# A decode step with grouped attention and a gated feed-forward: another order for the last loads, four strips for wo's last rows

## The chip, the cores and the metric

The kernel runs on one core of a Trainium2 chip. The metric is the device time of one execution in microseconds; each kernel is run several times and the median is given. A profile is one further execution with the hardware profiler on, and its times are counted from the start of its span.

## The reference

One token `x` (512 wide) goes through an attention block with a long cache and through a feed-forward block; a scalar gate mixes the two.

```python
q = x @ wq                                   # 32 heads of 128
k, v = k_cache, v_cache                      # 8 key/value heads, 32768 positions, 128 wide, bf16
scores = einsum(q, k) * 128 ** -0.5          # each k head serves 4 q heads
o = softmax(scores) @ v
a = o.reshape(4096) @ wo                     # wo: 4096 x 512
b = (silu(x @ w_gate) * (x @ w_up)) @ w_down # w_down: 1792 x 512
g = sigmoid((x * gate_w).sum())
out = g * a + (1 - g) * b                    # 512 numbers
```

Nearly all bytes are the two caches: 16 blocks of K and 16 blocks of V, of 4096 KB each.

## The kernel before

**Groups and blocks.** There are G = 8 groups (a key/value head with its four query heads), and each group's 32768 positions are NB = 2 blocks of 16384. Below, K(7,1) is the second block of K of the last group. A block is one DMA into one page of `page`: 128 partitions with 32 KB each. Pages 0 and 2 (`PG_K`) take the two K blocks of a group, pages 1 and 3 (`PG_V`) the V blocks; page 4 (`PG_X`) holds wq at first and wo later.

**TensorE** (line 314 on) first computes q, gate and up from wq, w_gate and w_up. Then a loop (line 509) runs G + 1 times; in turn i it does, for each block b, `emit_k` of group i (line 372: transposes K as 32-bit words into PSUM, DVE copies them to `ktT` at line 639, line 384 computes scores) and `emit_v` of group i - 1 (line 428: the exponentials times V, four at a time, into four strips of PSUM partitions of `ps_o`). `emit_v` of block 0 starts with `emit_reduce` (line 410), which sums the strips of the group before from `acc`, ACT's copy of `ps_o`. In the last turn there is no `emit_k`; between V(7,0) and V(7,1) `emit_warm` (line 466) runs 18 matmuls whose result nobody reads; behind V(7,1) comes `emit_end`.

**The end** (line 468 on): a matmul sums the exponentials, `emit_reduce` the last group. DVE scales (lines 662 to 668), transposes (675), TensorE permutes (479), DVE copies the result to `O2` (677): 32 columns, one for each of the 32 rows j of wo (each row is 128 partitions x 512 outputs). wo comes in five chunks (`WO_CUTS`, rows 0-8, 8-18, 18-26, 26-30, 30-32), each with its semaphore. The rows below `WIDE` = 18 go through `emit_wide` (line 440): one matmul with a stationary column and 512 moving columns, row j into strip j % 4 of `ps_w`. The 14 rows of w_down (with `tT`, the feed-forward's hidden vector, as columns) go the same way, between the first and the second chunk of wo. DVE copies `ps_w` to `part` (683). The remaining 14 rows of wo go through `emit_rows` (line 453), where a row is four matmuls with 128 moving columns each, one for each quarter of the 512 outputs; first the same is done with `part` and a column of ones (`sel5`), which adds up the four strips. The four quarters stand in two strips: each strip has two PSUM rows, and the stationary operand has two columns of which one is zero (`O2z`), so that a matmul adds to its own row and adds zero to the other. DVE casts the result to `res_row` (685), and SP and ACT store two rows of it each (205).

**The order of the loads** is the order in SP's program (line 279 on); all of them stand in one queue. A K block waits until its page's transposes are done (`sem_fill`), a V block until the V block before it in its page has been used (`sem_v_free`). At the end (lines 302 to 310) stand V(7,0), wo's first chunk, V(7,1), w_down, and wo's other four chunks.

Of the kernel before, what the change touches and what calls it, by code (L numbers as in the profile page):

```python
# [13 lines left out]
def bass_gated_mix__gqa_block_cached__swiglu_ffn__decode_kernel(  # L14
# [43 lines left out]
    assert KC * H * DH <= PAGE and 2 * KC * F <= PAGE and WOJ * NOUT <= PAGE  # L58
    WO_CUTS = [0, 8, 18, 26, 30, 32]
    KW = 1  # L60
    WIDE = WO_CUTS[KW + 1]
    NWARM = 18
    OC = NOUT // 128

    RQ = 4
    NSTRIP = 4
    RPS = 2
    assert RQ * HPG <= 32 and RQ * DH == 512

    PG_K = (0, 2)  # L70
# [5 lines left out]
    with ExitStack() as es:  # L76
# [83 lines left out]
        nbias = T("nbias", [128, G, HPG], FP32)  # L160
        esum = T("esum", [128, G, NB, HPG], FP32)
        esum2 = T("esum2", [128, G, HPG], FP32)
        sel5 = T("sel5", [128, 17], FP32)
        sel4 = sel5[:, 1:17]
        acc = T("acc", [128, RQ, DH], FP32)
        oT = T("oT", [128, (G + 2) * STEP], FP32)
        rS = T("rS", [128, H], FP32)
# [1 line left out]
        oTs = T("oTs", [128, H], BF16)  # L169
        O2a = T("O2a", [128, WOJ], BF16)  # L170
        O2 = T("O2", [128, WOJ], BF16)
        O2z = T("O2z", [128, WOJ - WIDE, RPS, RPS], BF16)
        part = T("part", [128, NOUT], FP32)
        res_row = T("res_row", [128, 128], BF16)

# [15 lines left out]
        ps_e = pst[0][:, 0:512]  # L191
        ps_c = pst[1][:, 0:512]
        ps_w = pst[0][:, 512:1024]
        ps_d = pst[1][:, 512:1024]

        def row_view(p):
            return page[:, p, :].rearrange("p (r d) -> p r d", d=DH)
# [5 lines left out]
        def store(eng, k):  # L203
            n = RPS * 128
            eng.dma_start(
                out[0, 0, n * k : n * (k + 1)].rearrange("(c n) -> c n", c=RPS),
                res_row[32 * k : 32 * k + RPS, :],
            ).then_inc(sem_out, 16)

        with nc.Block("main") as block:  # L210
# [48 lines left out]
            @block.sync  # L259
            def _(sp):  # L260
                def cache(which, g, b, p, sem):
                    sp.dma_start(
                        page[:, p, :].rearrange("p (r d) -> p r d", d=DH),
                        which[0, g, b * BLK : (b + 1) * BLK, :].rearrange("(p r) d -> p r d", r=R),
                    ).then_inc(sem, 16)
# [24 lines left out]
                load_v(0, 1)  # L290
                load_k(1, 1)
                for g in range(2, G):
                    for b in range(NB):
                        load_k(g, b)
                        load_v(g - 1, b)

                def load_wo(k):
                    a, b = WO_CUTS[k], WO_CUTS[k + 1]
                    src = A_wo.rearrange("(p j) n -> p j n", j=WOJ)
                    sp.dma_start(wo_v[:, a:b, :], src[:, a:b, :]).then_inc(sem_wo[k], 16)  # L300

                load_v(G - 1, 0)
                sp.wait_ge(sem_pe_q, 1)
                load_wo(0)
                load_v(G - 1, 1)
                sp.dma_start(
                    wd[:, :, :], B_w_down.rearrange("(p j) n -> p j n", j=FC)
                ).then_inc(sem_ld_wd, 16)
                for k in range(1, len(sem_wo)):
                    load_wo(k)  # L310
                sp.wait_ge(sem_dve_row, 1)
                store(sp, 0)

            @block.tensor
            def _(pe):
# [100 lines left out]
                        )  # L416
                    ins.then_inc(sem_red, STEP)

                def emit_v(i, b):
                    view = row_view(PG_V[b])  # L420
                    if b == 0:
                        emit_reduce(i)
                    pe.wait_ge(sem_page[PG_V[b]], i)
                    pe.wait_ge(sem_exp, i + 8 * (b + 1))
                    for k in range(R // RQ):
                        n = b * R + k * RQ
                        c = k % NSTRIP
                        ins = pe.matmul(  # L428
                            ps_o[32 * c : 32 * c + RQ * HPG, :],
                            ET[:, n : n + RQ, :].rearrange("p n h -> p (n h)"),  # L430
                            view[:, k * RQ : (k + 1) * RQ, :],
                            start=(b == 0 and k < NSTRIP),
                            stop=(b == NB - 1 and k >= R // RQ - NSTRIP),
                            skip_group_check=True,
                        )
                    ins.then_inc(sem_v_free, 1)
# [10 lines left out]
                    )  # L447

                def emit_rows(lhs, rhs, first, last):
                    for e in range(RPS):  # L450
                        for k in range(OC // RPS):
                            oc = RPS * k + e
                            ins = pe.matmul(  # L453
                                ps_c[32 * k : 32 * k + RPS, 0:128],
                                lhs(e),
                                rhs[:, oc * 128 : (oc + 1) * 128],
                                start=first and e == 0,
                                stop=last and e == RPS - 1,
                                skip_group_check=True,
                            )  # L460
                    return ins

                def emit_warm():
                    with pe.Fori(0, NWARM, 2):
                        for _ in range(2):
                            pe.matmul(ps_d, ident[:, :], ktT[:, 0, 0:512], start=True, stop=True)

                def emit_end():
                    pe.wait_ge(sem_dve_esum2, 1)
# [5 lines left out]
                        stop=True,  # L475
                    ).then_inc(sem_pe_S, 1)
                    emit_reduce((G + 1) * STEP)
                    pe.wait_ge(sem_dve_oT2, 1)
                    pe.matmul(
                        ps_m[:, M_O0 : M_O0 + WOJ], pmat[:, :], O2a[:, :], start=True, stop=True  # L480
                    ).then_inc(sem_pe_O2, 1)
                    pe.wait_ge(sem_dve_O2, 1)
                    for k, s in enumerate(sem_wo):
                        if k == 0:
                            pe.wait_ge(sem_psw, 1)
                        if k == 1:
                            pe.wait_ge(sem_dve_tT, 1)
                            pe.wait_ge(sem_ld_wd, 16)
                            for j in range(FC):
                                emit_wide(wd, tT, j, False, False)  # L490
                        pe.wait_ge(s, 16)
                        for j in range(WO_CUTS[k], WO_CUTS[k + 1]):
                            if j < WIDE:
                                ins = emit_wide(wo_v, O2, j, j < NSTRIP, j >= WIDE - NSTRIP)
                            else:
                                ins = emit_rows(
                                    lambda e: O2z[:, j - WIDE, e, :],
                                    wo_v[:, j, :],
                                    False,
                                    j == WOJ - 1,  # L500
# [1 line left out]
                        if k == KW:  # L502
                            ins.then_inc(sem_pe_w, 1)
                            pe.wait_ge(sem_dve_w, 1)
                            pe.wait_ge(sem_dve_oz, RPS)
                            emit_rows(lambda e: sel5[:, 1 - e : 3 - e], part, True, False)
                    ins.then_inc(sem_pe_sum, 1)

                with pe.Fori(0, (G + 1) * STEP, STEP) as i:
                    for b in range(NB):  # L510
                        with pe.If(i < G * STEP):
                            emit_k(i, b)
                        if b == NB - 1:
                            with pe.If(i > (G - 1) * STEP):
                                emit_warm()
                        with pe.If(i > 0):
                            emit_v(i, b)
                    with pe.If(i > (G - 1) * STEP):
                        emit_end()

            @block.scalar
# [45 lines left out]
            def _(dve):  # L567
# [21 lines left out]
                    sem_dve_gpart, 1  # L589
                )  # L590

                dve.memset(O2z[:, :, :, :], 0.0)
# [82 lines left out]
                dve.transpose(O2a[:, :], oTs[:, :]).then_inc(sem_dve_oT2, 1)  # L675
                dve.wait_ge(sem_pe_O2, 1)
                dve.tensor_copy(O2[:, :], ps_m[:, M_O0 : M_O0 + WOJ]).then_inc(sem_dve_O2, 1)
                for e in range(RPS):
                    dve.tensor_copy(
                        O2z[:, :, e, e], ps_m[:, M_O0 + WIDE : M_O0 + WOJ]  # L680
                    ).then_inc(sem_dve_oz, 1)
                dve.wait_ge(sem_pe_w, 1)
                dve.tensor_copy(part[:, :], ps_w[:, :]).then_inc(sem_dve_w, 1)  # L683
                dve.wait_ge(sem_pe_sum, 1)
                dve.tensor_copy(res_row[0 : 32 + RPS, :], ps_c[0 : 32 + RPS, 0:128]).then_inc(sem_dve_row, 1)  # L685


# [26 lines left out]
```

## Time and profile before

| What | us |
|---|---|
| median of 3 runs | 353.66 (353.34 to 355.68) |
| the profiled execution | 354.54 |
| its span, first to last instruction | 352.7 |
| TensorE busy | 274.8 |
| VectorE busy | 176.4 |
| ScalarE busy | 32.5 |

The granted TensorE clock was 0.855 of full speed in the mean. HBM was read at 420 GB/s over the span.

How to read the views: the page shows busy shares and a picture of the span in 40 slices of 8.8 us, each digit a share in tenths. The chain of waits follows the work that ended last back from the end: start, length, what it was. A timeline row has start and length of a run of equal instructions, engine, line, the shape (128\*16 means 128 rows and 16 columns of stationary operand), and in brackets the idle time before it with what ended it. A DMA row has the size of one DMA and the time from its issue to its landing. A row of windows has the stretch, its length, the engines' busy time, the granted clock, the share of the DMA engines, and GB/s. A row of a source line has the durations in ns (least, median, most) and the first and last start.

### The profile page before, as it was taken

What the parts mean: (1) busy time and instruction counts of PE and PEld (TensorE: products, weight loads), DVE (VectorE), ACT (ScalarE), POOL (GpSimd) and SP (SyncE); (2) the same over time, 40 slices, a digit from 0 to 9 for tenths busy, and PEclk for the clock granted to TensorE, in tenths of its full rate; (3) what the DMA queues carried; (4) which work ended last, traced back from release to release, by engine and by line L of the source; (5) the groups of instructions that cost most, each with busy time, mean ns of one, the idle gap of its engine ahead of it and who ended that gap; (6) DMA issues with size and microseconds to landing.
All of it is one profiled execution on the core that took longest, in us unless ns stands there. A gap on an engine that the chain in (4) does not pass through costs nothing.

```text
span 352.7 us, 8976 instructions
## 1 busy us (share of the span) xinstructions
PE 274.8 (78%) x4014; PEld 233.6 (66%) x4023; DVE 176.4 (50%) x194; ACT 32.5 (9%) x148; POOL 6.9 (2%) x29
## 2 busy tenths in 40 slices
PE   0446986997999969695896959894988969796676
PEld 0436986967787949394876849592968668493234
DVE  0011967655674949074653828192645637282011
ACT  1000000400130040003000040004000220004000
POOL 4000000000000000000000000000000000000000
PEclk9999989687898999789885989588787889698776
DMA  8999999999999999999999999999999999999993
GB/s 338 404 445 422 451 429 414 423 442 438 416 435 435 438 416 439 435 435 420 438 431 435 424 438 435 427 427 438 438 420 431 435 438 420 438 435 431 414 415 122
DMA packets 5924, 148.23 MB, mean 420 GB/s; under 512 B 666, under 2 KB 668, under 8 KB 924
## 3 DMA queue, kind: packets, MB, share of 16 engines
q1 hardware_dynamic: 5912, 148.12, 98.0%
q8 instruction: 6, 0.10, 0.1%
q14 instruction: 2, 0.02, 0.0%
q10 hardware_dynamic: 4, 0.00, 0.0%
HBM read 148.11 MB, written 0.00 MB: 420 GB/s over the span
## 4 chain that ended last, share of the span: by engine, by line
DMA 58%; PE 37%; DVE 3%; issue 1%; SPq 1%; ACT 0%; DVEq 0%; ACTq 0%
DMA page<-in_A_k_cache_dram 53%; PE pst L372 25%; PE ps_sc L384 6%; DMA page<-in_A_v_cache_dram 5%; PE ps_o L428 3%; DVE ktT L639 2%; PE pst L453 1%; PE pst L440 1%; PE ps_m L410 1%; SPq L283 0%; DVE part L683 0%; ACT acc L554 0%; SPq L279 0%; SPq L280 0%; DVE res_row L685 0%
## 5 line engine op out<-in xcount | busy, mean ns | idle before, releaser
L639 DVE COPY ktT<-pst 128x2048 bf16<-128x2048 bf16 x128 | 155.8, 1224 | 105.5 <-PE pst L372 98.5
L372 PE MATMUL pst<-ident_f,page 128*128 128x128 f32 x1024 | 157.1, 310 | 38.6 <-DMA page<-in_A_k_cache_dram 36.7
L372 PEld LDWEIGHTS pst<-ident_f,page 128*128 128x128 f32 x1024 | 133.7, 161 | 50.6 <-DMA page<-in_A_k_cache_dram 45.0
L384 PE MATMUL ps_sc<-qcur,ktT 128*128 128x8 bf16 x2048 | 67.8, 166 | 8.6 <-DVE ktT L639 8.6
L384 PEld LDWEIGHTS ps_sc<-qcur,ktT 128*128 128x128 bf16 x2048 | 66.9, 97 | 11.3 <-DVE ktT L639 10.0
L428 PE MATMUL ps_o<-page,ET 128*16 128x512 bf16 x512 | 44.6, 509 | 3.4 <-DMA page<-in_A_v_cache_dram 3.3
L428 PEld LDWEIGHTS ps_o<-page,ET 128*16 128x16 bf16 x512 | 14.2, 107 | 22.8 <-issue 16.4
L533 ACT ACTIVATE nbias<-gmax 128x4 f32<-128x4 f32 x8 | 1.6, 205 | 261.7 <-POOL gmax L254 261.7
L542 ACT ACTIVATE ET<-ps_sc,nbias 128x128 bf16<-128x128 f32 x64 | 24.3, 552 | 0.7
L542 ACT ACTIVATION_READ_ACCUMULATOR ET<-ps_sc,nbias 128x1 f32 x64 | 18.0, 281 | 0.0
L644 DVE TENSOR_REDUCE pmaxf<-ps_sc 128x4 f32<-128x512 f32 x16 | 11.1, 692 | 11.5 <-PE ps_sc L384 11.5
L410 PE MATMUL ps_m<-sel,acc 128*128 128x4 f32 x72 | 10.7, 271 | 3.6 <-ACT acc L554 3.6
L410 PEld LDWEIGHTS ps_m<-sel,acc 128*128 128x128 f32 x72 | 10.0, 216 | 4.2 <-ACT acc L554 4.2
L358 PE MATMUL ps_m<-xT,page 128*128 128x1 bf16 x112 | 6.9, 198 | 5.2 <-DMA page<-in_B_w_up_dram 5.2
L321 PE MATMUL ps_m<-ones_bf,x_row 1*128 1x1 bf16 x4 | 0.3, 173 | 12.9 <-DMA gw_row<-in_gate_w_dram 12.9
L358 PEld LDWEIGHTS ps_m<-xT,page 128*128 128x128 bf16 x112 | 6.8, 160 | 5.3 <-DMA page<-in_B_w_up_dram 5.3
L254 POOL PARTITION_ALL_REDUCE gmax<-pmax x8 | 3.0, 373 | 301.7 <-DVE pmax L646 301.7
L321 PEld LDWEIGHTS ps_m<-ones_bf,x_row 1*128 1x128 bf16 x4 | 0.2, 115 | 12.9 <-DMA gw_row<-in_gate_w_dram 12.9
L662 DVE RECIPROCAL rS<-pst 128x32 f32<-128x32 f32 x1 | 0.4, 358 | 15.3 <-PE pst L470 15.3
L554 ACT ACTIVATE acc<-ps_o 128x512 f32<-128x512 f32 x8 | 5.2, 646 | 16.8 <-PE ps_o L428 16.8
L579 DVE CAST xT<-ps_m 128x4 bf16<-128x4 f32 x1 | 0.2, 161 | 11.9 <-PE ps_m L321 11.9
L618 DVE TENSOR_TENSOR t<-sg,ps_m 128x14 f32<-128x14 f32 x1 | 0.2, 171 | 11.0 <-ACT sg L527 11.0
(65 smaller groups left out, 44.8 us busy)
## 6 DMA issues: line engine op xcount, KB each, us to landing
page<-in_A_k_cache_dram SPq DMA_DIRECT2D x16, 4096.0 KB, 27.2
page<-in_A_v_cache_dram SPq DMA_DIRECT2D x16, 4096.0 KB, 31.1
page<-in_A_wq_dram SPq DMA_DIRECT2D x1, 4096.0 KB, 12.4
page<-in_A_wo_dram SPq DMA_DIRECT2D x2, 1024.0 KB, 24.5
page<-in_B_w_gate_dram SPq DMA_DIRECT2D x1, 1792.0 KB, 15.6
page<-in_B_w_up_dram SPq DMA_DIRECT2D x1, 1792.0 KB, 20.8
wd<-in_B_w_down_dram SPq DMA_DIRECT2D x1, 1792.0 KB, 20.6
page<-in_A_wo_dram SPq DMA_DIRECT2D x1, 1280.0 KB, 23.3
```

The costliest lines, as they stand in the source:

```text
L254: pool.partition_all_reduce(gmax[:, g, :], pmax[:, g * STEP : g * STEP + HPG], 128, ReduceOp.max).then_inc(sem_gmax, 1)
L358: ins = pe.matmul(ps_m[:, base + j : base + j + 1], wgu[:, w, c, :].rearrange("d (p j) -> d j p", j=FC)[:, j, :], xT[:, c : c + 1], start= ...
L372: ins = pe.transpose(pst[u % NST][:, k * 128 : (k + 1) * 128], kv[:, n * 128 : (n + 1) * 128], ident_f[:, :],)
L384: ins = pe.matmul(ps_sc[b][:, col : col + 2 * HPG], kt[:, k, e, :], qcur[:, e, :], start=(e == 0), stop=(e == 1),)
L410: ins = pe.matmul(ps_m[:, M_P0 : M_P0 + HPG], acc[:, q, :], sel4[:, q * HPG : (q + 1) * HPG], start=(q == 0), stop=(q == RQ - 1),)
L428: ins = pe.matmul(ps_o[32 * c : 32 * c + RQ * HPG, :], ET[:, n : n + RQ, :].rearrange("p n h -> p (n h)"), view[:, k * RQ : (k + 1) * RQ, ...
L440: return pe.matmul(ps_w[32 * c : 32 * c + 1, :], vec[:, j : j + 1], w[:, j, :], start=first, stop=last, skip_group_check=True,)
L453: ins = pe.matmul(ps_c[32 * k : 32 * k + RPS, 0:128], lhs(e), rhs[:, oc * 128 : (oc + 1) * 128], start=first and e == 0, stop=last and e = ...
L542: act.activation(ET[:, b * R : (b + 1) * R, h], sc[:, h, :], ACT.Exp, bias=nbias[:, g, h : h + 1], scale=SCALE, accum_out=esum[:, g, b, h ...
L554: act.activation(acc[:, :, :].rearrange("p q d -> p (q d)"), ps_o[:, :], ACT.Copy).then_inc(sem_acc, STEP)
L639: dve.tensor_copy(ktT[:, u % NKT, :], pst[u % NST][:, :].bitcast(BF16)).then_inc(sem_cp, 1)
L644: dve.tensor_reduce(pmaxf[:, b, :], sc, AX.X, ALU.max).then_inc(sem_pmax, 4)
```

## The change

- V(7,1) goes into page 0, a K page, instead of page 3. SP waits for the transposes of K(7,0) instead of the use of V(6,1), and issues it right behind V(7,0); w_down and then all five chunks of wo follow.
- In TensorE's loop `emit_v` of block 1 stands under the condition of `emit_k`; the last V block, from its new page, is written out behind the loop's blocks. `emit_warm` is gone.
- `emit_rows` puts the four quarters into four strips. Quarters 0 and 2 use a stationary operand of 32 columns of which only the last is not zero, so that the result stands in the last row of strip 0 or 2; quarters 1 and 3 use one column, so that it stands in the first row of strip 1 or 3. The rows of one store (31 and 32, 95 and 96) remain neighbours. `O2z` and `sel5` grow, one copy on DVE replaces two, and the final cast covers 128 partitions instead of 34.
- The first eight of w_down's 14 matmuls move ahead of the permutation of O2; they begin the sums in `ps_w`.

```diff
+    WD_CUT = 8
-    NWARM = 18
+    SW = 32
...
-        sel5 = T("sel5", [128, 17], FP32)
-        sel4 = sel5[:, 1:17]
+        sel5 = T("sel5", [128, SW + 15], FP32)
+        sel4 = sel5[:, SW - 1 : SW + 15]
...
-        O2z = T("O2z", [128, WOJ - WIDE, RPS, RPS], BF16)
+        O2z = T("O2z", [128, WOJ - WIDE, SW], BF16)
...
-                res_row[32 * k : 32 * k + RPS, :],
+                res_row[64 * k + SW - 1 : 64 * k + SW + 1, :],
...
                 load_v(G - 1, 0)
-                sp.wait_ge(sem_pe_q, 1)
-                load_wo(0)
-                load_v(G - 1, 1)
+                sp.wait_ge(sem_fill, UPG * (G - 1) + UPP)
+                cache(A_v_cache, G - 1, 1, PG_K[0], sem_page[PG_K[0]])
                 sp.dma_start(
                     wd[:, :, :], B_w_down.rearrange("(p j) n -> p j n", j=FC)
                 ).then_inc(sem_ld_wd, 16)
-                for k in range(1, len(sem_wo)):
+                sp.wait_ge(sem_pe_q, 1)
+                for k in range(len(sem_wo)):
                     load_wo(k)
...
-                    for e in range(RPS):
-                        for k in range(OC // RPS):
-                            oc = RPS * k + e
-                            ins = pe.matmul(
-                                ps_c[32 * k : 32 * k + RPS, 0:128],
-                                lhs(e),
-                                rhs[:, oc * 128 : (oc + 1) * 128],
-                                start=first and e == 0,
-                                stop=last and e == RPS - 1,
-                                skip_group_check=True,
-                            )
+                    for oc in range(OC):
+                        e = oc % RPS
+                        ins = pe.matmul(
+                            ps_c[32 * oc : 32 * oc + (1 if e else SW), 0:128],
+                            lhs(e),
+                            rhs[:, oc * 128 : (oc + 1) * 128],
+                            start=first,
+                            stop=last,
+                            skip_group_check=True,
+                        )
...
                     emit_reduce((G + 1) * STEP)
+                    pe.wait_ge(sem_dve_tT, 1)
+                    pe.wait_ge(sem_ld_wd, 16)
+                    pe.wait_ge(sem_psw, 1)
+                    for j in range(WD_CUT):
+                        emit_wide(wd, tT, j, j < NSTRIP, False)
...
-                            for j in range(FC):
+                            for j in range(WD_CUT, FC):
                                 emit_wide(wd, tT, j, False, False)
...
-                                    lambda e: O2z[:, j - WIDE, e, :],
+                                    lambda e: O2[:, j : j + 1] if e else O2z[:, j - WIDE, :],
...
-                            emit_rows(lambda e: sel5[:, 1 - e : 3 - e], part, True, False)
+                            emit_rows(lambda e: sel5[:, SW - 1 : SW] if e else sel5[:, 0:SW], part, True, False)
...
                         with pe.If(i < G * STEP):
                             emit_k(i, b)
-                        if b == NB - 1:
-                            with pe.If(i > (G - 1) * STEP):
-                                emit_warm()
-                        with pe.If(i > 0):
-                            emit_v(i, b)
+                            if b:
+                                with pe.If(i > 0):
+                                    emit_v(i, b)
+                        if b == 0:
+                            with pe.If(i > 0):
+                                emit_v(i, b)
                     with pe.If(i > (G - 1) * STEP):
+                        emit_v(G * STEP, 1, PG_K[0], (G + 1) * STEP)
                         emit_end()
...
-                for e in range(RPS):
-                    dve.tensor_copy(
-                        O2z[:, :, e, e], ps_m[:, M_O0 + WIDE : M_O0 + WOJ]
-                    ).then_inc(sem_dve_oz, 1)
+                dve.tensor_copy(
+                    O2z[:, :, SW - 1], ps_m[:, M_O0 + WIDE : M_O0 + WOJ]
+                ).then_inc(sem_dve_oz, 1)
...
-                dve.tensor_copy(res_row[0 : 32 + RPS, :], ps_c[0 : 32 + RPS, 0:128]).then_inc(sem_dve_row, 1)
+                dve.tensor_copy(res_row[:, :], ps_c[:, 0:128]).then_inc(sem_dve_row, 1)
```

More of the change, by code (lines that the diff above doesn't have):

```diff
@@ L193, in bass_gated_mix__gqa_block_cached__swiglu_ffn__decode_kernel @@
         ps_w = pst[0][:, 512:1024]
-        ps_d = pst[1][:, 512:1024]
         def row_view(p):
@@ L417, in emit_reduce, with emit_v @@
                     ins.then_inc(sem_red, STEP)
-                def emit_v(i, b):
-                    view = row_view(PG_V[b])
+                def emit_v(i, b, pg=None, landed=None):
+                    pg = PG_V[b] if pg is None else pg
+                    view = row_view(pg)
                     if b == 0:
                         emit_reduce(i)
-                    pe.wait_ge(sem_page[PG_V[b]], i)
+                    pe.wait_ge(sem_page[pg], i if landed is None else landed)
                     pe.wait_ge(sem_exp, i + 8 * (b + 1))
@@ L449, in emit_rows @@
                 def emit_rows(lhs, rhs, first, last):
-                    for e in range(RPS):
-                        for k in range(OC // RPS):
-                            oc = RPS * k + e
-                            ins = pe.matmul(
-                                ps_c[32 * k : 32 * k + RPS, 0:128],
-                                lhs(e),
-                                rhs[:, oc * 128 : (oc + 1) * 128],
-                                start=first and e == 0,
-                                stop=last and e == RPS - 1,
-                                skip_group_check=True,
-                            )
-                    return ins
[L463 to L466, printed above, removed]
+                    for oc in range(OC):
[8 more added lines that the diff above has]
+                        )
+                    return ins
                 def emit_end():
@@ L483, in emit_end @@
                     for k, s in enumerate(sem_wo):
-                        if k == 0:
-                            pe.wait_ge(sem_psw, 1)
                         if k == 1:
-                            pe.wait_ge(sem_dve_tT, 1)
-                            pe.wait_ge(sem_ld_wd, 16)
-                            for j in range(FC):
+                            for j in range(WD_CUT, FC):
                                 emit_wide(wd, tT, j, False, False)
@@ L493, in emit_end @@
                             if j < WIDE:
-                                ins = emit_wide(wo_v, O2, j, j < NSTRIP, j >= WIDE - NSTRIP)
+                                ins = emit_wide(wo_v, O2, j, False, j >= WIDE - NSTRIP)
                             else:
                                 ins = emit_rows(
-                                    lambda e: O2z[:, j - WIDE, e, :],
+                                    lambda e: O2[:, j : j + 1] if e else O2z[:, j - WIDE, :],
                                     wo_v[:, j, :],
@@ L504, in emit_end @@
                             pe.wait_ge(sem_dve_w, 1)
-                            pe.wait_ge(sem_dve_oz, RPS)
-                            emit_rows(lambda e: sel5[:, 1 - e : 3 - e], part, True, False)
+                            pe.wait_ge(sem_dve_oz, 1)
+                            emit_rows(lambda e: sel5[:, SW - 1 : SW] if e else sel5[:, 0:SW], part, True, False)
                     ins.then_inc(sem_pe_sum, 1)
@@ L590, in _ @@
                 )
-                dve.memset(O2z[:, :, :, :], 0.0)
+                dve.memset(O2z[:, :, :], 0.0)
                 dve.wait_ge(sem_pe_q, 1)
```

## The prediction

> **What bounds the kernel now.** I read the page first (busy shares, slices, queues), then the timeline of SP's queue with the landings of its DMAs, then the chain of waits from its end backwards, then single rows of TensorE in the last 30 us.
>
> ```profile
> PE 274.8 (78%) x4014; PEld 233.6 (66%) x4023; DVE 176.4 (50%) x194; ACT 32.5 (9%) x148; POOL 6.9 (2%) x29
> DMA  8999999999999999999999999999999999999993
> q1 hardware_dynamic: 5912, 148.12, 98.0%
> ```
>
> No engine is full, but the DMA slices are, from the second to the last but one: 148.12 MB are moved and the change moves the same bytes. So the kernel is a stream of bytes with a tail. The change can touch only the tail, unless it opens a hole in the stream. These are the last DMAs that SP issues, and after them the landings (issue to landing, by size):
>
> ```profile
> 302.51 0.33 SPq L262 DMA_DIRECT2D page<-in_A_v_cache_dram  x1
> 302.89 0.43 SPq L300 DMA_DIRECT2D page<-in_A_wo_dram  x1
> 319.62 0.33 SPq L262 DMA_DIRECT2D page<-in_A_v_cache_dram  x1
> 319.99 0.43 SPq L306 DMA_DIRECT2D wd<-in_B_w_down_dram  x1
> 320.47 1.85 SPq L300 DMA_DIRECT2D page<-in_A_wo_dram  x4
> ```
>
> ```profile
> page<-in_A_v_cache_dram SPq DMA_DIRECT2D x1, 4096.0 KB, 21.6
> page<-in_A_wo_dram SPq DMA_DIRECT2D x1, 1024.0 KB, 23.7
> ...
> page<-in_A_v_cache_dram SPq DMA_DIRECT2D x1, 4096.0 KB, 16.7
> wd<-in_B_w_down_dram SPq DMA_DIRECT2D x1, 1792.0 KB, 20.6
> page<-in_A_wo_dram SPq DMA_DIRECT2D x1, 1280.0 KB, 23.3
> page<-in_A_wo_dram SPq DMA_DIRECT2D x1, 1024.0 KB, 25.3
> page<-in_A_wo_dram SPq DMA_DIRECT2D x1, 512.0 KB, 26.0
> page<-in_A_wo_dram SPq DMA_DIRECT2D x1, 256.0 KB, 26.2
> ```
>
> Issue plus landing time gives the landings: V(7,0) at 302.51 + 21.6 = 324.1; wo's first chunk at 302.89 + 23.7 = 326.6; V(7,1) at 336.3; wd at 340.6; wo's second chunk at 343.8. The four last wo issues start (1.85 - 0.43) / 3 = 0.47 apart, so wo's third, fourth and fifth chunks land at 320.94 + 25.3 = 346.2, 321.42 + 26.0 = 347.4 and 321.89 + 26.2 = 348.1. The landings follow each other at the pace of their bytes: 9.7 us for V's 4096 KB, 2.5 us for 1024 KB, 4.3 us for wd. V(7,1) was issued only at 319.62, but 7 us before the queue ahead of it was done (326.6), so that wait costs the stream nothing. **The last byte lands at 348.1; the span is 352.7.**
>
> The end of the chain of waits (start, length, what):
>
> ```profile
> 319.62 16.72 DMA page<-in_A_v_cache_dram
> 336.34 0.12 issue
> 336.46 3.24 PE ps_o L428 x32
> ...
> 339.77 0.61 ACT acc L554
> ...
> 340.42 1.07 PE ps_m L410 x8
> ...
> 342.30 0.20 PE ps_m L479
> ...
> 342.53 0.20 DVE O L677
> ...
> 342.78 3.14 PE pst L440 x32
> ...
> 345.94 0.70 DVE part L683
> ...
> 346.69 4.01 PE pst L453 x64
> 350.70 0.02 issue
> 350.73 0.28 DVE res_row L685
> ```
>
> The chain leaves the stream at 336.34, with V(7,1), and is compute from there on: no wo or wd landing ends a wait. TensorE's last matmul ends at 350.70, 2.6 us after the last byte is there. What can be won is this lag, and no more.
>
> **The change part by part.** *TensorE's prices in the tail.* Rows of the timeline, then of single lines and of windows (the third number from a window's end is the granted clock):
>
> ```profile
> 325.03 0.14 PEld L428 LDWEIGHTS ps_o<-page,ET 128*16 128x16 bf16 x4 [0.28 <-issue]
> 325.46 0.14 PEld L428 LDWEIGHTS ps_o<-page,ET 128*16 128x16 bf16 x4 [0.28 <-issue]
> ...
> 346.69 1.02 PE L453 MATMUL pst<-part,sel 128*2 128x128 f32 x8 [0.79 <-DVE part L683]
> ...
> 347.50 3.19 PE L453 MATMUL pst<-page,O2z 128*2 128x128 bf16 x56
> ```
>
> ```profile
> L453 PE MATMUL pst<-page,O2z x56: 301/314/314, 347.5 to 350.4; 128*2 128x128 bf16 x56
> L440 PE MATMUL pst<-page,O x18: 377/634/634, 342.8 to 345.3; 128*1 128x512 bf16 x18
> 327.00:328.00 1.00, 1.00 (x12) 0.50 0.99 426
> 336.90:340.20 3.30, 3.30 (x30) 0.50 0.97 408
> 343.70:350.50 6.80, 6.01 (x84) 0.50 0.43 172
> ```
>
> At a granted clock of 0.50, four matmuls of 512 columns in four strips start together, and the next four 0.43 us later (the loads at 325.03 and 325.46): 0.107 us for each 128 columns. The wo rows use two strips: 56 matmuls in 28 pairs, (3.19 - 0.31) / 27 = 0.107 us a pair, 0.213 us a row of wo. So a step costs its columns, however many strips run in it.
>
> *V(7,1) into page 0.* Page 0 is free when K(7,0) is transposed, which in TensorE's program precedes V(6,0), whose end let V(7,0) go at 302.51; so the new wait on SP is met when SP gets there. V(7,1) follows V(7,0) in the queue, wd and all of wo behind it, all issued by about 306. V(7,1) lands at 324.1 + 9.7 = 333.8 (2.5 earlier), wd at 338.1, wo's first chunk at 340.6 (14 us later than before), the other chunks where they were: 343.8, 346.2, 347.4, 348.1. The sum of bytes ahead of the last is the same, and so is the last landing. Behind SP's new wait stand wd and wo, so if it were met late, all of them would be; at 302.9 it is long met. Their place in the queue has no other user.
>
> *V(7,1)'s chain.* All at the clock of 0.50: matmuls from 333.95 for 8 x 0.43 + 0.2 = 3.6, to 337.6; then as in the chain above (339.70 to 341.49, 1.8 us) the esum matmul, ACT's copy and the reduction, to 339.4. wd has been there since 338.1, so the eight w_down matmuls moved ahead, two steps of 0.43, run beside DVE's part, which before took 0.8 us (341.49 to 342.30); I charge 0.1. Behind their wait for wd stand the O2 matmul and all of wo, but wd is 1.3 us early. O2 is ready at 339.4 + 0.9 + 0.5 = 340.8, with wo's first chunk there at 340.6. Its two steps and the six other w_down matmuls (two steps) take 1.7 us, to 342.5: 1.3 us before wo's second chunk, at 343.8. This chain is covered by that landing.
>
> *Unread matmuls.* They ran from 328 to 333 in TensorE's idle time. Without them V(7,1) starts at half clock, but in the trace most of it did already (0.50 from 336.9 to 340.2), and the sum above has it all at 0.50. Worth nothing either way, with 1.3 us to spare; if that cover went, a slow V(7,1) would be next to be late.
>
> *From wo's second chunk.* Start at 343.8 + 0.1; ten wide matmuls, the last two starting 2 x 0.43 later, and 0.63 long: 345.4. DVE's copy, 0.05 + 0.70: 346.1. The part matmuls: before eight records over 1.02 us in two strips; in four strips 346.15 + 0.2 + 0.4 = 346.7 for the end, and the rows follow from 346.6. Their stationary operand is now 32 columns wide in half of them. No row shows such a load in f32, and I bound the surplus by 0 and by the whole 1.02 us of the old group; I take 0, since the 16-column loads above (0.14 us for four) fit into a step with room to spare. Rows of the third chunk: 8 x 0.107 = 0.9, to 347.5, when the fourth chunk has landed (347.4 + 0.1): 4 x 0.107, to 347.9. **Fifth chunk: landed 348.1, start 0.12 later (V's wait above), second row 0.107 later, 0.31 long: 348.65.** Then 0.03 + 0.28 for the cast, which reads 128 partitions instead of 34, with 128 elements in each as before: 348.96, against 350.73 + 0.28 = 351.01. The stores are of the same size, and the rest stays at 352.7 - 351.0 = 1.7.
>
> *Elsewhere.* One O2z copy fewer on DVE, and a larger memset in the first 13 us, both beside the stream, as is the nested condition in TensorE's loop (a branch in each turn). Thirty-two more matmuls stand in the program in place of the warm loop: the code came in six pieces,
>
> ```profile
> q8 instruction: 6, 0.10, 0.1%
> ```
>
> and one more piece would be 0.017 MB, 0.04 us of the stream if shared by all its engines, 0.6 us if one engine carries it alone.
>
> **Sum:** 348.96 - 351.01 = -2.05 us. The profiled execution took 354.54 us, 0.9 above the median of 353.66; taken off the median, this gives 351.6.
>
> **The rivals.** (1) *The rows do not go four at a time* but stay at pairs, say because the 32-column load takes a strip's gap: part ends as before (0.8 for its starts), 14 rows x 0.213 = 3.0 us from 346.95 end at 350.2: a gain of 0.5, 353.2. For it: no row has a mix of 32 and 1 columns. Against it: four strips with 16 columns work.
>
> (2) *Slower: the loads are not hidden at all*, and each of the four matmuls of a row waits for its own load, one step of 0.107 each: a row costs 0.43 instead of 0.213. Part 8 x 0.107 from 346.15, to 347.0; 14 x 0.43 = 6.0, plus 0.2 for the last: 353.2, against 350.7 before: +2.5, 356.2. It decides from (350.5 - 346.6) / 14 = 0.28 us a row. The trace is against it: four loads start within 0.14 us at 325.03, while the matmuls of the step before still run (377 to 634 ns long, 0.43 apart). The Trainium skill, "TensorE: Matmul & The Clock Gate", Part 3, The mechanism, has a rule that would bring this: a load overlaps matmuls in flight only where its row group differs, and all four strips here use all 128 rows. By that rule the sum would be 356.2; by the rows it is 351.6; the rows at 325 disagree with the rule for column strips, so I give it little.
>
> (3) *V(7,1) is not earlier*, because SP's new wait or the queue holds it. Then O2 is ready 2.5 later, at about 343.2; wo's first chunk and w_down until 344.9, ten wide matmuls until 346.4, copy 347.1, part 347.6, 14 rows x 0.107 = 1.5, end 349.3: a gain of 1.4, 352.3. So the strips carry most of the gain, the early V the rest.
>
> (4) *A hole in the stream*: any delay of the last landing goes one for one into the end. For it only the new order; against it, each landing followed the one before by its bytes.
>
> **How the numbers follow.** Forecast -2.05: 0.70, own range 350.8 to 352.4 (faster clock at the end or slower part matmuls). Rival 1: 0.11, at 353.2. Rival 2: 0.05, at 356.2. Rival 3: 0.06, at 352.3. Rival 4 and the unforeseen: 0.08, both sides. The range 350.6 to 353.5 takes in the forecast and rivals 1 and 3. A measurement of this kernel tells about 1%, 3.5 us, from no change. The forecast and the first three rivals lie within it, 0.92, less 0.05 for what I cannot size; faster by over 1% (under 350.1) would need the stream itself to be shorter, 0.05; slower (over 357.2) needs rival 4 or a worse rival 2, 0.08.
>
> **What would show it.** V(7,1) issued near 303 and landed near 333.8; wo's last chunk landed near 348.1, and the chain leaving the stream there instead of at V. The wo rows in fours 0.107 apart; TensorE idle before each of the last four chunks. The cast's start near 348.7. The prediction is wrong if the last landing is elsewhere than 347.5 to 348.7, if rows are over 0.2 us apart, or if a wait other than a landing ends TensorE's idle time after 343.

## The result, and the profile after

| | median us | runs from | to |
|---|---|---|---|
| before, 11 runs | 353.88 | 353.34 | 355.68 |
| after, 11 runs | 352.50 | 352.27 | 352.77 |

The ratio is 0.9954, 95% interval 0.9941 to 0.9968: 1.4 us less. The profiled executions differ by more, 354.54 and 352.48, and the scatter has gone: 2.3 us before, 0.5 after. The experiments below trace both to the clock in TensorE's tail. One run of the strips alone took 384.9 us at a granted clock of 0.59 in the mean, against 0.84 to 0.88 in all other runs here, and is left out of that experiment's numbers. First the profile after, the last loads on SP's queue and their landings:

```profile
302.85 0.80 SPq L262 DMA_DIRECT2D page<-in_A_v_cache_dram  x2
303.69 0.43 SPq L305 DMA_DIRECT2D wd<-in_B_w_down_dram  x1
304.17 2.33 SPq L300 DMA_DIRECT2D page<-in_A_wo_dram  x5
```

```profile
wd<-in_B_w_down_dram SPq DMA_DIRECT2D x1, 1792.0 KB, 34.5
...
page<-in_A_wo_dram SPq DMA_DIRECT2D x1, 512.0 KB, 41.9
page<-in_A_wo_dram SPq DMA_DIRECT2D x1, 256.0 KB, 42.1
```

Everything is issued by 306.5. wd lands at 303.69 + 34.5 = 338.2, wo's last chunk at 304.17 + 2.33 - 0.43 + 42.1 = 348.2: the stream is as long as before (348.1). The end of the chain of waits:

```profile
304.64 39.11 DMA page<-in_A_wo_dram
343.75 0.04 issue
343.79 1.46 PE pst L441 x9
...
345.28 0.70 DVE part L680
...
346.02 1.50 PE pst L453 x38
...
347.55 0.61 PE pst L453 x14
...
348.19 0.43 PE pst L453 x4
...
348.65 0.29 DVE res_row L682
```

The chain now leaves the loads at wo's second chunk (343.75), 7.4 us later than before, and the starts of the last two pieces of TensorE, 347.55 and 348.19, are the landings of the last two chunks: rows start 0.107 apart, but 0.35 passes between the last row of the fourth chunk (347.84) and the first of the fifth. The third chunk's rows wait for no landing; they wait for DVE's copy of `part`. The cast starts at 348.65, the predicted number; before it was 350.73. TensorE's rows behind it, and a row of windows over the tail (the granted clock is the third number from the end):

```profile
333.93 3.59 PE L429 MATMUL ps_o<-page,ET 128*16 128x512 bf16 x32 [4.65 <-DMA page<-in_A_v_cache_dram]
...
341.23 0.84 PE L441 MATMUL pst<-wd,tT 128*1 128x512 bf16 x6
343.79 1.44 PE L441 MATMUL pst<-page,O 128*1 128x512 bf16 x10 [1.72 <-DMA page<-in_A_wo_dram]
...
346.45 0.33 PE L453 MATMUL pst<-page,O2z 128*32 128x128 bf16 x2
...
346.52 0.33 PE L453 MATMUL pst<-page,O 128*1 128x128 bf16 x2
...
346.56 0.33 PE L453 MATMUL pst<-page,O2z 128*32 128x128 bf16 x2
```

```profile
341.50:348.70 7.20, 4.53 (x80) 0.50 0.70 287
```

V(7,1) is there at 333.9. The chain of V(7,1) ends 1.72 us before wo's second chunk (the bracket at 343.79), so it is covered. In the rows two 32-column and two one-column matmuls fall into 0.107 us (346.45 to 346.56): four strips at once, at a granted clock of 0.50.

### The profile page after: what moved, and what is told of

It reads as the page before. It is cut to its first block, busy times and chain, and to the rows that moved or that the text cites. A ratio compares the mean times of both kernels' runs of the same rounds, so it can differ in the third digit from the quotient of the medians.

```text
span 350.7 us, 8919 instructions
## 1 busy us (share of the span) xinstructions
PE 269.5 (77%) x4005; PEld 232.4 (66%) x4005; DVE 176.9 (50%) x193; ACT 32.1 (9%) x148; POOL 6.9 (2%) x29
## 4 chain that ended last, share of the span: by engine, by line
DMA 64%; PE 31%; DVE 2%; SPq 1%; issue 1%
DMA page<-in_A_k_cache_dram 53%; PE pst L372 23%; DMA page<-in_A_wo_dram 11%; PE ps_sc L384 5%; DVE ktT L637 2%; PE ps_o L429 1%; PE pst L453 1%; PE pst L441 0%; PE ps_m L410 0%; SPq L283 0%; SPq L262 0%; DVE part L680 0%; SPq L305 0%; SPq L300 0%; SPq L279 0%
## 5 line engine op out<-in xcount | busy, mean ns | idle before, releaser
L372 PE MATMUL pst<-ident_f,page 128*128 128x128 f32 x1024 | 160.2, 315 | 40.2 <-DMA page<-in_A_k_cache_dram 38.8
L372 PEld LDWEIGHTS pst<-ident_f,page 128*128 128x128 f32 x1024 | 137.2, 164 | 50.6 <-DMA page<-in_A_k_cache_dram 46.7
L429 PE MATMUL ps_o<-page,ET 128*16 128x512 bf16 x512 | 42.1, 487 | 4.6 <-DMA page<-in_A_v_cache_dram 4.6
L429 PEld LDWEIGHTS ps_o<-page,ET 128*16 128x16 bf16 x512 | 13.3, 104 | 23.2 <-issue 10.7
## 6 DMA issues: line engine op xcount, KB each, us to landing
wd<-in_B_w_down_dram SPq DMA_DIRECT2D x1, 1792.0 KB, 34.5
```

The costliest lines, as they stand in the source:

```text
L372: ins = pe.transpose(pst[u % NST][:, k * 128 : (k + 1) * 128], kv[:, n * 128 : (n + 1) * 128], ident_f[:, :],)
L429: ins = pe.matmul(ps_o[32 * c : 32 * c + RQ * HPG, :], ET[:, n : n + RQ, :].rearrange("p n h -> p (n h)"), view[:, k * RQ : (k + 1) * RQ, ...
```

## The experiments

All times are medians in us; the kernel before ran beside each of the three groups, on the chip of that group, 81 times in all, from 352.3 to 356.8. The whole change did not run there again: its 352.50 is that of the result above.

**The strips alone.** The kernel before, with the change's `emit_rows`, its operands, the cast and the stores.

```diff
-                    for e in range(RPS):
-                        for k in range(OC // RPS):
...
+                    for oc in range(OC):
+                        e = oc % RPS
```

> Before, with the four strips alone (old order of loads, unread matmuls kept, w_down whole). My theory: the strips carry most of the gain. Part's sum ends TensorE's wait at 346.7 as before; its matmuls take 0.4 us until the rows follow, the 14 rows 0.107 each at half clock, so the last matmul ends at about 348.9 instead of 350.7: 1.8 us off a run whose tail is at half clock, 0.3 short of the whole change; median 352.6 to 352.9. The rival, that the early V block and the new order carry it: under 0.5 us, median above 353.4.

Measured: 352.71 (352.3 to 355.0), ratio to before 0.9979 (0.9954 to 1.0005). The median is where it was expected, but the interval still holds no change, and the profiled run (354.01) shows what the working had left out:

```profile
336.61 3.62 PE ps_o L429 x32
...
340.95 1.89 PE ps_m L411 x8
...
344.14 4.02 PE pst L441 x32
...
348.18 0.70 DVE part L682
...
348.93 1.23 PE pst L453 x60
```

In this execution the reduction takes 1.89 instead of 1.07 us and the wide matmuls 4.02 instead of 3.14, so part's copy starts at 348.18 instead of 345.94; the granted clock was 0.50 from 336 to 348.2. The chain from V(7,1)'s landing to that copy is nearly 12 us long, and its parts depend on the clock granted just then.

**The order alone.** The whole change without the strips.

```diff
+                    for e in range(RPS):
+                        for k in range(OC // RPS):
...
-                    for oc in range(OC):
-                        e = oc % RPS
```

> The whole change without the four strips: rows in pairs, 0.213 us a row at half clock. My theory: part's sum is ready at 346.0 as in the whole change, the rows run from 346.8 to about 350.1 at half clock, so 0.6 us less than before in a like run; where the clock is full in the tail, the rows keep up with the landings and the time is that of the whole change. Median 352.9 to 353.5. The rival, that the order carries the gain: 352.5 to 352.7.

Measured: 353.95 (353.03 to 354.83), ratio 1.000 (0.9973 to 1.0026): no gain, a miss by 0.5 to 1 us. The profiled run (353.50), TensorE's last rows:

```profile
346.03 1.02 PE L453 MATMUL pst<-part,sel 128*2 128x128 f32 x8 [0.79 <-DVE part L681]
346.83 2.81 PE L453 MATMUL pst<-page,O2z 128*2 128x128 bf16 x56
```

The rows begin at 346.83 as worked out, and the clock became full only at 349.1. With half clock to the end they would end at 346.83 + 27 x 0.107 + 0.31 = 350.0, 1.4 later than in the whole change: 353.9, the median. I had counted on a full clock in part of the runs. So neither half shows a gain clear of the scatter: the order alone gives none in the median, the strips alone 0.84, within an interval that holds no change. The order buys time ahead of the rows, the strips halve the rows, and with both the end comes down to the last landing: the eleven runs of the whole change lie within 0.5 us.

**The kernel before, once more.**

> The kernel before once more, for its profile. Its 11 runs lie between 353.3 and 355.7, those of the changed kernel between 352.3 and 352.8. My theory: the stream's last landing is at 348.1 again within 0.2 us, and what varies is the clock in TensorE's tail, so a run that is shorter than 354.5 shows rows closer than 0.213 us each. The rival: the clock in the tail is the same and the stream's end moves.

Measured (one execution): 353.13, 1.4 less than the first profiled run of the same code. Its chain, and the clock in its last windows (third number from the end):

```profile
342.64 3.71 PE pst L440 x30
...
346.37 0.70 DVE part L683
...
347.12 2.19 PE pst L453 x64
```

```profile
344.00:347.00 3.00, 2.33 (x24) 0.69 0.81 326
347.00:350.00 3.00, 2.17 (x64) 1.00 0.05 18
```

The same 64 matmuls take 2.19 us at full clock, against 4.01 at 0.50. The last landing is at 347.9 here, 0.2 earlier. So what differs between these two executions of the kernel before is the clock in its tail, and the first profiled one was a slow draw of it: the medians differ by 1.4 and the profiled runs of before and after by 2.1. The whole scatter fits this, as an estimate: with half clock throughout, part's copy would start 2.24 later, as with the strips alone (348.18 against 345.94), which makes 354.54 into 356.8, the longest run there is; the shortest, 352.3, is the time of the whole change. Neither of these two ends was profiled.

**Wide unread matmuls in the tail of before.** Four ahead of O2's matmul, five ahead of part's.

```diff
+                    for _ in range(4):
+                        pe.matmul(ps_d, ident[:, :], ktT[:, 0, 0:512], start=True, stop=True)
                     pe.wait_ge(sem_dve_oT2, 1)
```

> Before, with nine more unread matmuls of 128 columns of stationary operand in TensorE's two waits of the tail (four ahead of O2's matmul, five ahead of part's). If wide matmuls bring the full clock where the one- and two-column matmuls did not, the 28 pairs of rows go from 0.107 to 0.056 us each, 1.4 us less, against up to 0.9 us for the unread matmuls themselves where they outlast the wait: last matmul at 349.3 to 350.4, median 352.8 to 353.6. If the clock stays at half, they only delay: last matmul at 351 or later, median 354 or more.

Measured: 354.14, ratio 1.0002 (0.9966 to 1.0038). The median misses the range by 0.5 us, and the run is inconclusive: the rows did run at full clock,

```profile
346.95 1.19 PE pst L507 x5
348.13 2.11 PE pst L453 x64
```

but they do so without them too, in the run above, and the five matmuls held them up to 348.13. What brings the full clock stays open.

**384 KB more, in both kernels.** A load that nobody reads, ahead of wo's last chunk.

```diff
+                    if k == len(sem_wo) - 1:
+                        load_junk()
                     load_wo(k)
```

> The whole change, and 384 KB more, which nobody reads, loaded ahead of wo's last chunk. My theory: the end hangs on the last landing, so the time grows by these bytes at the stream's pace, 384 / 4096 x 9.7 = 0.91 us, and some 0.05 for one more DMA: 353.3 to 353.7, with as little scatter as the whole change had. Rival, that compute ends last: the slack of the chain takes it, under 0.3 us.

> The kernel before, with the same 384 KB at the same place. My theory: TensorE comes to wo's last chunk only at 348.9 (full clock in the rows) to 350.2 (half clock), and the chunk now lands at 349.1: 0 to 0.3 us, within the scatter, median 353.4 to 354.2. Rival, that the stream ended the kernel before: 0.9 to 1.0 us more, 354.5 or above.

Measured: the whole change 353.64, 1.14 more than its 352.50; the kernel before 353.83, against 353.82 beside it (ratio 0.9997, 0.9968 to 1.0026). The profiled run of the whole change with the load:

```profile
306.42 42.65 DMA page<-in_A_wo_dram
349.07 0.04 issue
349.11 0.43 PE pst L463 x4
```

The last landing moves from 348.15 to 349.07, 0.92, and the end with it: the spans of the twelve runs lie between 351.6 and 351.9, against 350.5 to 350.8 without the load. So the end is the stream's now. In the median of the kernel before the same bytes are free, though the upper end of the interval, 0.9 us, is about their price. And they are not free in every run: in the profiled one (353.45) the clock was full, 1.00 from 347 to 350, and the end follows the last landing there too:

```profile
323.44 25.66 DMA page<-in_A_wo_dram
349.10 0.04 issue
349.14 0.41 PE pst L463 x8
```

No run of before with the load is under 353.4; nine of the 29 without it are. So the kernel before ends with the later of the two: with compute in most runs, with the stream in its fastest, and the change takes it to that floor in all of them.

**The unread matmuls kept.** `emit_warm` again, between the last two V blocks.

```diff
+                        emit_warm()
                         emit_v(G * STEP, 1, PG_K[0], (G + 1) * STEP)
```

> The whole change with the 18 unread matmuls kept, between V(7,0) and V(7,1). My theory: they run in TensorE's idle time and the chain has 1.3 us to spare before wo's second chunk, so 352.3 to 352.7, no difference. Rival, that leaving them out matters: if they keep the clock full, under 352.2; if they run into V(7,1), 352.9 or more.

Measured: 353.85 (352.52 to 354.17), 1.35 more than without them, though one of the ten runs, 352.52, is as fast as without. The theory falls here. The tail looks as it should (V(7,1) even runs at full clock, 1.90 us), but the last load's row is

```profile
305.81 2.33 SPq L302 DMA_DIRECT2D page<-in_A_wo_dram  x5
```

```profile
page<-in_A_wo_dram SPq DMA_DIRECT2D x1, 256.0 KB, 42.1
```

so it lands at 349.8, not 348.15: the stream itself has a hole of 1.65 us. Going back along SP's queue, the first difference is at 60 us, where the loop returns for the first time. In the whole change and with the unread matmuls kept, TensorE's first transposes after it:

```profile
62.83 5.38 PE L372 MATMUL pst<-ident_f,page 128*128 128x128 f32 x24 [3.01 <-DMA page<-in_A_k_cache_dram]
```

```profile
67.89 4.93 PE L374 MATMUL pst<-ident_f,page 128*128 128x128 f32 x24 [7.12 <-issue]
```

and SP's next two K blocks, in the same order (the second is issued 0.33 before the end of the row):

```profile
57.97 17.17 SPq L262 DMA_DIRECT2D page<-in_A_k_cache_dram  x2
```

```profile
58.93 20.82 SPq L264 DMA_DIRECT2D page<-in_A_k_cache_dram  x2
```

TensorE stands for 7.12 us, "issue": it waits for no engine and no load that the profile shows, while its block of K landed at 61.8. Most of that time goes to one branch, the one that jumps over the end's code in all turns but the last (`with pe.If(i > (G - 1) * STEP)`). Of its nine executions the first is the longest, at 59.6 and 60.6 (the numbers are the least, the median and the most in ns):

```profile
L515 PEldq COMPARE_BRANCH  x9: 73/207/2378, 59.6 to 326.4; - x9
```

```profile
L522 PEldq COMPARE_BRANCH  x9: 73/208/6537, 60.6 to 327.0; - x9
```

Everything behind it is late; SP issues K(2,0) at 79.4 instead of 74.8, and there the queue runs dry: the windows from 78 to 80 and from 80 to 82 us show 279 and 262 GB/s, against 442 and 475 in the whole change. The queue of instructions (q8) carries pieces of 16 KB; two of them, at 60.9 and 64.5, fall into TensorE's wait. So the guess: it waits for code, and the unread matmuls matter as code, 60 us after the start, not as work, at 330.

**Code inside the loop, code behind it, less code.** Three kernels for that guess: 16 small unread matmuls at the end of the loop's last turn; the same 16 behind the loop's return; the unread matmuls kept, with w_down's 14 left out.

```diff
                         emit_end()
+                        for _ in range(16):
+                            pe.matmul(ps_d[:, 0:8], ident[:, :], ktT[:, 0, 0:8], start=True, stop=True)
```

> The whole change, and 16 small unread matmuls at the very end of the loop's last turn, behind the matmul that everything waits for: 32 more instructions of code inside the loop, run only beside the stores. Theory C: keeping the unread matmuls cost 1.35 us because TensorE's code got longer (the loop's first return, at 60 us, waited 6.6 us for code there, against 2.4 in the whole change), and a hole in the stream followed; so this costs the same: a long wait at 60 us, the last landing at about 349.8, 353.4 to 354.2. Rival: it was the unread matmuls in TensorE's idle time themselves; then this makes no difference, 352.3 to 352.8.

> The same 16 matmuls, but behind the loop's return branch. Theory C in its narrow form, that the loop's own length decides: no wait at 60 us, 352.3 to 352.8. In its wide form, that the length of the whole program decides: as with the code inside the loop, 353.4 to 354.2.

> The 18 unread matmuls kept, but w_down's 14 matmuls left out (the feed-forward's part is missing from the sum), so the code is 28 instructions shorter and shorter than that of the whole change. Theory C: the short wait at 60 us comes back, the last landing is at 348.1, 352.3 to 352.7, although the unread matmuls run. Rival, the unread matmuls themselves: 353.4 to 354.2.

Measured: 353.73 inside the loop, 352.65 behind it, 352.53 with the unread matmuls kept and less code. TensorE's first transposes after the return, in this order:

```profile
66.65 4.43 PE L373 MATMUL pst<-ident_f,page 128*128 128x128 f32 x24 [7.16 <-issue]
```

```profile
62.10 5.38 PE L373 MATMUL pst<-ident_f,page 128*128 128x128 f32 x24 [2.37 <-DMA page<-in_A_k_cache_dram]
```

```profile
63.13 5.38 PE L374 MATMUL pst<-ident_f,page 128*128 128x128 f32 x24 [2.24 <-issue]
```

All three come out as the narrow form of the theory has it: code ahead of the loop's return costs, the same code behind it does not, and the unread matmuls cost nothing where the loop is short enough. Two things stay argued. The code was added and left out within the block that the waiting branch jumps over, so the length of the loop and the length of that block are not told apart; and that TensorE waits for code is read from the pieces that fall into the wait, not tested by itself.

**w_down in one piece.**

```diff
-    WD_CUT = 8
+    WD_CUT = 0
```

> The whole change with w_down's 14 matmuls in one piece at their old place, between wo's first and second chunk. The prediction's working: TensorE is then idle in DVE's 0.8 us, and the 14 matmuls take 3.5 steps of 0.43 us from 341.6 on, until about 343.2 at half clock; wo's second chunk lands at 343.75, so nothing changes: 352.3 to 352.7. Rival, that the split is part of the gain: 352.9 or more.

Measured: 354.27, 1.8 more: a miss, but not for the rival's reason. The same hole is there, with the same matmuls in another order:

```profile
69.03 3.25 PE L372 MATMUL pst<-ident_f,page 128*128 128x128 f32 x14 [8.25 <-issue]
...
307.27 42.91 DMA page<-in_A_wo_dram
350.17 0.04 issue
350.22 0.43 PE pst L453 x4
```

Here the branch over the end's code takes 1.62 us, and the rest of the wait lies just behind it, at the return branch itself: the loop's counter is raised at 62.3, and the branch starts at 68.4. The end still hangs on the last landing (350.17), which is 2.0 late; so the split of w_down could not show a price in the tail here, and that it is worth nothing there remains as worked out. In the loop's first turn none of the end's code runs, so its order cannot matter there; its length can. The pages count 8919 instructions in the whole change and 8920 here: the matmuls are as many, and the one more is a semaphore wait of TensorE's that stands by itself in the end's code (26 of them against 25). So the whole change lies one instruction from the long wait. Keeping the unread matmuls added seven: two matmuls, each with its load, and the three instructions of their loop.

**Which DMA engines are late.** Two small loads behind wo's last chunk.

```diff
+                for n, i, sem in ((8, 0, sem_j8), (24, 1, sem_j12)):
+                    sp.dma_start(junk[0:n, i, :], ...
```

> The whole change, and behind wo's last chunk two DMAs of 8 and 24 rows of 512 bytes, which nobody reads. Each landing in the traces is spread over 1.8 us, from the first DMA engine to the last: six engines are done 1.6 us before the last ones. The counts of these small DMAs show whether the late engines are among the first eight or the first twelve. Time: 0.1 to 0.2 us more than the whole change, 352.6.

Measured (one execution): 352.44. Of the eight counts of the smaller load one is late (348.2, the others 346.5 to 347.6), of the twelve of the larger three. If the counts stand for the first eight and the first twelve engines, the late ones are spread over both groups, and giving the last bytes to fewer engines would put them on a late one as well; no kernel was made of it.

## Why the prediction was right, and where it was not

*What bounds it*: right. The last landing is at 348.1 before and 348.15 after, and what could be won was the lag behind it; the extra 384 KB move the end after, and not the median before.

*V(7,1) into page 0*: right. Landed at 333.9 (333.8 worked out), wd at 338.2, no wait of SP's.

*V(7,1)'s chain and its cover*: right in its times: O2's users start at 340.8, TensorE is idle from 342.1 to 343.8. But the working says "all at the clock of 0.50" and takes the 1.8 us of reduction and DVE from a stretch of the kernel before whose granted clock was 0.93 (340 to 344); in the profile after it was 0.93 there as well (337.5 to 341.4), so it fits. At half clock the reduction takes 1.89 us instead of 1.07, as the strips alone show, which would use up 0.8 of the 1.7 us of cover. Rival 3 priced a late V(7,1) from the one profiled run, whose wide matmuls began at a fuller clock; with the strips alone, half clock up to there, and w_down whole, part's copy ran from 348.2, not from 346.4 as rival 3 had it. What the early V covers depends on the clock of the run.

*The rows*: right. Four at a time, 0.107 us a row; rival 1 and rival 2 are out. The rule quoted there from the Trainium skill ("TensorE: Matmul & The Clock Gate", Part 3, The mechanism), that a load overlaps matmuls in flight only where its row group differs, does not hold for these column strips, if it is taken alone: all four use all 128 rows, and a row cost 0.107 us, not 0.43.

*The strips carry most of the gain*: not clear. Alone they gave 0.84 us in the median, within an interval that holds no change; the order alone gave none; both gave 1.4.

*The sum*: -2.05 us against -2.06 between the two profiled runs, and -1.38 between the medians. The measured 352.50 lies in the whole range, but 0.1 above the forecast's own (350.8 to 352.4), and next to rival 3's 352.3; rival 3 is out all the same, since V(7,1) landed at 333.9. The step that was mis-sized is "taken off the median". The end before was in most runs compute's and moved with the clock, the end after is the stream's and does not; so a lag read from a slow draw, 2.05, was taken off a median whose own lag is smaller, about 1.4 by the difference measured. Set from the profiled run, 354.54 - 2.05 = 352.5, the same working gives the measured median.

*The signs*: V(7,1) was issued and landed as named, the last landing, the rows and the cast's start too. TensorE is not kept waiting by each of the last four chunks: the third had landed at 346.2 and its rows waited for `part`. So one wait after 343 ends with DVE's copy (346.02) and not with a landing. The list counts that as a sign of being wrong, while the working itself has the copy there, until 346.1: the list was worded too widely.

*The unread matmuls, "worth nothing either way"*: wrong as a step, by 1.35 us, though not in their time in the tail. *One more piece of code*, priced at 0.04 to 0.6 us as bytes of the stream: wrong mechanism. A seventh piece was fetched in the changed kernel as well, at 349.9, and cost nothing; the price is TensorE's wait at the end of the loop's first turn, for code as far as the runs show, and the hole that follows, 1.65 us. The change repeats 32 matmuls of a V block inside the loop, and stays on the cheap side by one instruction, as w_down in one piece shows. The prediction did not look at this: its 0.08 for a hole in the stream named only the new order, and that the change got past it was luck.

Open: why the tail gets the full clock in one execution of the kernel before and the half clock in another; whether the loop's length or that of the block jumped over brings the long wait; and why single runs of the kernels with the long wait, 352.52 and 352.50, were as fast as those without.

## What to carry to other kernels

When a saturated stream sets the floor, find the last landing and the lag from there to the end; the lag is all there is to win, and once the end follows the last landing, the scatter that the clock brings goes too. If the new end is tied to the stream, count the new time from the stream's end, not from the median of a kernel whose lag varies. Two halves of a tail change can each look worthless alone; and code added to a long loop can have a price at the end of the loop's first turn, far from the place where it runs.

## What the runs showed of the hardware

The same tail code of the kernel before ran its last 64 matmuls in 4.01 us in one execution, at a granted clock of 0.50, and in 2.19 us in another, at 1.00. TensorE was idle 2.15 to 3.39 us ahead of the first transposes behind its loop's first turn in the profiles of the kernels with the shorter loop, and 7.12 to 8.25 us in the three with the longer one, with pieces of 16 KB on the instruction queue in that time. The Trainium skill, "Runtime: NRT & Kernel Launch", Instruction fetch mechanics, says that a taken branch to code that is not in the window held forces a fetch before execution goes on. With the unread matmuls kept and with code inside the loop the wait agrees: it is the time of such a branch, 6.5 us, paid in the first turn alone (the median of the nine is 0.21 us). With w_down in one piece it does not lie at that branch (1.62 us) but one instruction behind its target.
